# Score columns laid out by head, and batched Q/K rows in 128x32 tiles

## The chip, the cores and the metric

The kernel runs on one core of one Trainium2 chip. A core has a matrix engine (TensorE; PE in the profile, with its weight loads as PEld), three engines that work on tensors (VectorE or DVE, ScalarE or ACT, GpSimd or POOL) and a sync engine (SP) that issues most DMAs. Matmuls read SBUF and write PSUM, 128 partitions of eight banks with 512 float32 columns each; DVE and ACT bring results back to SBUF. Each engine takes its own list of instructions in order, and waits on semaphores for the others. The metric is the device time of one execution in microseconds (us).

## The reference

Two sublayers follow each other, x of shape 2048 x 512 in bfloat16. The first is attention over 64 segments of 32 rows, with a memory of 8 rows that each segment hands to the next; the second is a gated MLP that mixes rows (`_B_ref`).

```python
for s in range(n_seg):                       # 64 segments, one after the other
    xs = x[:, s * seg_len:(s + 1) * seg_len, :]
    h = concatenate([mem, xs], axis=1)       # 8 + 32 = 40 rows
    q, k, v = (einsum('btd,dhe->bhte', h, W) for W in (Wq, Wk, Wv))   # 32 heads of 128
    scores = einsum('bhqe,bhke->bhqk', q, k) * scale
    scores = where(mask, scores, -1e9)       # key < 8 or key <= query
    o = einsum('bhqk,bhke->bhqe', softmax(scores), v)
    o = einsum('bhte,hed->btd', o, Wo)
    mem = o[:, :8, :]                        # needed by the next segment
    outs.append(o[:, 8:, :])
h = x + concatenate(outs); h2 = h + _B_ref(layernorm(h), ...)
```

The memory rows make the segments sequential. All of q, k, v, the scores and the output projection of a segment's recurrent part stand on this path.

## The kernel before

Every operation is added to one list with the buffers that it reads and writes; from these the semaphore waits follow, and each engine gets its operations in the order in which they were added. So the order of the calls in the loop over segments (`for s in range(NSEG)`, L869) is the order of the work on every engine.

A segment's 40 rows are split in two groups. The first 32 (8 memory rows and the segment's first 24) are "main"; the last 8 are "extra". The extra rows do not depend on the memory, so their Q, K and V are computed in batches of 16 segments (a chunk): `qkx_mm` (L403) for Q and K, `vx_mm` (L424) for V. Chunks 0 and part of chunk 1 are done before the loop and in its first segment. The rest is spread over the loop: the list `gx` holds groups of matmuls, and each segment takes one (L942) and puts it between its V matmuls and its PV matmuls. Segments 0 to 7, 14 and 15 take a V group (L430), segments 8 to 13 and 16 to 47 a Q/K group (L411), and from segment 49 on it is a piece of the second sublayer (L725). A Q/K group has 4 heads x 4 pieces of the contraction = 16 matmuls, each with a full 128x128 weight block and 128 columns; its result is copied out by DVE (L422) after the copies of PV.

In the loop most matmuls use a quarter of the array's columns: weights of 128 rows and 32 columns, four such tiles side by side (`tile_position=(0, 32 * c)`), the four writing to the four groups of 32 partitions of one bank. The profile gives these as 128*32. PV uses the other split, 32 rows and 128 columns (32*128). The order on PE in a segment:

1. Q and K of the main rows (L481) for both halves b of the heads; ACT copies each to `Tst` (L488), and DVE transposes it to `QT` and `KT` (L494, L497).
2. `S_half(s, 0)`: for four groups of partitions c, a matmul that writes the mask (L511, identity times `mask`), then scores of main keys (L520), then scores of the extra keys (L526), all into one bank. ACT takes the exponential (L534) into `E_sb`.
3. V of half 0 (L575, 16 matmuls), then the sums of half 0 (L541 for main keys, L546 for extra keys; the matrix `ones` sums over partitions). ACT turns the sums into reciprocals by a logarithm (L553) and an exponential (L557).
4. `S_half(s, 1)`, three quarters of V of half 1 (12 matmuls of L575), the sums of half 1, the last quarter of V (4 matmuls). ACT copies V of half 1 (L582); DVE multiplies `E_sb` by the reciprocals (L561 main keys, L566 extra keys) for both halves.
5. The group from `gx`. Then PV of half 0 and half 1 (L592 main keys, L598 extra keys).
6. PV's results are copied to `cT`; the output projection follows (L625, with L676 for the extra rows of earlier segments), then the memory rows of the next segment (L649, L654).

In the score bank the 224 columns of a half lie in two blocks: columns 0 to 159 hold main keys, 40 queries for each of 4 heads; columns 160 to 223 hold extra keys. Extra keys are needed only for 16 queries of a head (the extra rows and the memory rows), 4 x 16 = 64 columns. `mask` has the same 224 columns, and the mask matmul, which opens the sum in the bank, covers them all.

## Time and profile before

| | us |
|---|---|
| median of 3 runs (lowest, highest) | 892.15 (890.42, 892.38) |
| the profiled execution | 891.1 |
| span of its instructions | 889.4 |
| PE busy | 862.0 |
| DVE busy, ACT busy, POOL busy | 487.4, 455.5, 110.7 |

The granted clock of the profiled execution is 0.994 of full speed. A row of a timeline has start, length, engine, line, operation, output and input tiles, shapes and the count of merged instructions; in brackets stands the idle time of the engine before it and what ended it ("issue" where nothing in the profile was waited for). A matmul's end is modelled, and matmuls overlap, so times between starts tell more than lengths. A row by stretches has from and to, the length, then for PE, PEld, DVE, ACT and POOL the busy time and the number of instructions, the granted clock, the share of the DMA engines and GB/s. A row on a DMA queue has the queue, its kind, packets, MB and the share of the DMA engines.

### The profile page before, as it was taken

To read this page: it belongs to the slowest core of one execution; us is meant where nothing else is said; L and a number is where in the kernel's file an instruction comes from. 1 tells how busy PE (TensorE), PEld (TensorE's weight loads), DVE (VectorE), ACT (ScalarE), POOL (GpSimd) and SP (SyncE) were. 2 spreads that over 40 slices of the span, in tenths; PEclk is the share of its full clock that TensorE was granted. 3 is DMA by queue.
4 is the path that set the end of the run, shared out by engine and by line. 5 is a ranking of instruction groups with operands and counts; after the bars stand their busy time and mean duration, and the time that the engine had idled before them with its cause. 6 is when DMAs were issued, how large, how long until landed. Compare 5 with 4: busy or idle time off the path is not lost.

```text
span 889.4 us, 46102 instructions
## 1 busy us (share of the span) xinstructions
PE 862.0 (97%) x21213; PEld 487.0 (55%) x21213; DVE 487.4 (55%) x1127; ACT 455.5 (51%) x1145; POOL 110.7 (12%) x280
## 2 busy tenths in 40 slices
PE   6889999999999999999999999999999979999997
PEld 6645555555656555656665655555555534444443
DVE  3445556565656556565656565555555546464443
ACT  2346566666665666666665666565566655400000
POOL 1420111111111111010101111111101013100000
PEclk9999999999999999999999999999999999999999
DMA  9962222222320311211212122432221296032101
GB/s 326 376 180 52 63 57 60 43 60 63 60 58 25 83 45 37 60 54 43 60 42 57 49 61 79 73 73 67 65 61 56 76 273 227 1 100 76 62 13 38
DMA packets 106312, 74.55 MB, mean 84 GB/s; under 512 B 62360, under 2 KB 91616, under 8 KB 106112
## 3 DMA queue, kind: packets, MB, share of 16 engines
q1 hardware_dynamic: 105600, 71.27, 28.8%
q8 instruction: 168, 2.75, 1.3%
q14 instruction: 32, 0.26, 0.1%
q0 software_dynamic: 192, 0.20, 0.1%
q10 hardware_dynamic: 320, 0.07, 0.0%
HBM read 41.07 MB, written 20.22 MB: 69 GB/s over the span
## 4 chain that ended last, share of the span: by engine, by line
PE 93%; DVE 2%; DMA 2%; issue 1%; POOL 1%; ACT 0%; SPq 0%; DVEq 0%
PE f_ps L481 26%; PE f_ps L625 13%; PE f_ps L575 12%; PE f_ps L1064 11%; PE f_ps L411 7%; PE f_ps L676 4%; PE f_ps L592 3%; PE f_ps L430 3%; PE f_ps L1153 3%; PE f_ps L1057 2%; PE f_ps L725 2%; PE f_ps L520 2%; PE f_ps L541 1%; PE f_ps L511 1%; DMA f_arena<-in_B_w_in_dram 1%; PE f_ps L649 1%
## 5 line engine op out<-in xcount | busy, mean ns | idle before, releaser
L481 PE MATMUL f_ps<-f_arena,f_hT 128*32 128x512 bf16 x4096 | 240.5, 380 | 1.0 <-issue 0.4
L488 ACT ACTIVATE f_Tst<-f_ps 128x512 bf16<-128x512 f32 x256 | 145.9, 596 | 78.6 <-PE f_ps L481 78.3
L481 PEld LDWEIGHTS f_ps<-f_arena,f_hT 128*32 128x32 bf16 x4096 | 93.6, 96 | 104.6 <-ACT f_hT L654 33.3
L575 PE MATMUL f_ps<-f_arena,f_hT 128*32 128x512 bf16 x2048 | 140.4, 378 | 0.0
L625 PE MATMUL f_ps<-f_arena,f_cT 128*32 128x256 bf16 x4096 | 127.4, 272 | 0.8 <-ACT f_cT L611 0.8
L625 PEld LDWEIGHTS f_ps<-f_arena,f_cT 128*32 128x32 bf16 x4096 | 99.8, 96 | 24.1 <-ACT f_cT L611 22.1
L494 DVE STREAM_TRANSPOSE f_QT<-f_Tst 128x256 uint32<-128x256 uint32 x128 | 57.0, 445 | 92.4 <-ACT f_Tst L488 92.4
L1064 PE MATMUL f_ps<-f_arena 128*128 128x512 bf16 x448 | 100.1, 379 | 0.0
L613 DVE TENSOR_SCALAR f_cT<-f_ps 128x320 bf16<-128x320 f32 x128 | 56.9, 486 | 39.7 <-PE f_ps L598 39.7
L497 DVE STREAM_TRANSPOSE f_KT<-f_Tst 128x256 uint32<-128x256 uint32 x128 | 57.0, 445 | 29.1 <-ACT f_Tst L488 26.3
L1064 PEld LDWEIGHTS f_ps<-f_arena 128*128 128x128 bf16 x448 | 43.7, 98 | 52.6
L411 PE MATMUL f_ps<-f_hTe,f_arena 128*128 128x128 bf16 x1024 | 68.2, 225 | 4.2 <-DVE f_arena L422 3.2
L411 PEld LDWEIGHTS f_ps<-f_hTe,f_arena 128*128 128x128 bf16 x1024 | 60.6, 101 | 14.1 <-issue 9.2
L504 POOL COPY f_QT<-f_arena 128x256 bf16<-128x256 bf16 x64 | 30.8, 481 | 298.7 <-PE f_ps L526 298.6
L611 ACT ACTIVATE f_cT<-f_ps 128x320 bf16<-128x320 f32 x128 | 49.0, 435 | 36.8 <-PE f_ps L598 36.8
L561 DVE SCALAR_TENSOR_TENSOR f_E_sb<-f_R_sb,f_E_sb 128x160 bf16<-128x160 f32 x128 | 41.6, 325 | 46.3 <-ACT f_R_sb L557 46.3
L642 DVE CAST f_part<-f_ps 128x256 bf16<-128x256 f32 x64 | 27.2, 424 | 67.0 <-PE f_ps L625 67.0
L553 ACT ACTIVATE f_R_sb<-f_ps 128x160 f32<-128x160 f32 x128 | 38.8, 303 | 38.1 <-PE f_ps L546 38.1
L575 PEld LDWEIGHTS f_ps<-f_arena,f_hT 128*32 128x32 bf16 x2048 | 45.1, 95 | 21.1
L654 ACT ACTIVATE f_hT<-f_ps 128x16 bf16<-128x16 f32 x126 | 23.1, 183 | 55.4 <-PE f_ps L649 55.1
L633 POOL COPY f_cTx<-f_cT 128x256 bf16<-128x256 bf16 x64 | 25.6, 401 | 195.6 <-DVE f_cT L613 195.6
L1070 DVE TENSOR_TENSOR f_arena<-f_ps,f_arena 128x512 f32<-128x512 f32 x28 | 19.3, 689 | 55.8 <-PE f_ps L1064 55.8
(106 smaller groups left out, 1160.3 us busy)
## 6 DMA issues: line engine op xcount, KB each, us to landing
wT_d<-f_wst SPq DMA_DIRECT2D x32, 256.0 KB, 2.1
f_arena<-wT_d SPq DMA_DIRECT2D x32, 256.0 KB, 5.1
f_arena<-in_A_Wq_dram SPq DMA_DIRECT2D x4, 1024.0 KB, 8.5
f_arena<-in_A_Wk_dram SPq DMA_DIRECT2D x4, 1024.0 KB, 14.1
f_arena<-in_A_Wv_dram SPq DMA_DIRECT2D x4, 1024.0 KB, 14.5
f_arena<-in_A_Wo_dram SPq DMA_DIRECT2D x4, 1024.0 KB, 13.6
f_Vx<-vext_d SPq DMA_DIRECT2D x62, 64.0 KB, 2.8
vext_d<-f_Vs SPq DMA_DIRECT2D x24, 128.0 KB, 2.0
```

What stands on the lines that cost most here:

```text
L411: pe(lambda e, h=h, dc=dc, hh=hh: e.matmul(ps[:, bank, hh * 128:(hh + 1) * 128], lhsT=ws[:, dc, h * DH:(h + 1) * DH], rhs=hTe[:, ck % 3, d ...
L481: pe(lambda e, dc=dc, c=c, rhs=rhs: e.matmul(ps[32 * c:32 * c + 32, bank, :], lhsT=hT[:, sl, dc, :], rhs=rhs, start=(dc == 0), stop=(dc == ...
L488: act(lambda e: e.activation(out=Tst[:, tb, :].rearrange("p (hp i r) -> p hp i r", i=32, r=2), in_=ps[:, bank, :].rearrange("p (hp r i) -> ...
L494: dve(lambda e: e.transpose(out=dst, in_=src), reads=[("T", tb)], writes=[("QT", b)])
L497: dve(lambda e: e.transpose(out=dst, in_=src), reads=[("T", tb)], writes=[("KT", b)])
L553: act(lambda e: e.activation(out=R_sb[:, b, :], in_=ps[:, bank, 224:384], func=ACT.Ln, scale=LNS), reads=[PB(bank)], writes=[("R", b)])
L561: dve(lambda e: e.scalar_tensor_tensor(out=E_sb[:, b, 0:160], in0=R_sb[:, b, :], scalar=RK, in1=E_sb[:, b, 0:160], op0=ALU.mult, op1=ALU.m ...
L575: pe(lambda e, dc=dc, c=c, c0=c0: e.matmul(ps[32 * c:32 * c + 32, bank, :], lhsT=hT[:, sl, dc, :], rhs=w_v[:, dc, c0:c0 + 512], start=(dc ...
L611: act(lambda e: e.activation(out=dst, in_=src, func=ACT.Copy, scale=UNSC), reads=[PB(PVB[c])], writes=[("cT", c)])
L613: dve(lambda e: e.tensor_scalar(out=dst, in0=src, scalar1=UNSC, scalar2=None, op0=ALU.mult), reads=[PB(PVB[c])], writes=[("cT", c)])
L625: pe(lambda e, h=h, g=g, i=i, b=b, c=c: e.matmul(ps[32 * g:32 * g + 32, bank, 0:d1 - d0], lhsT=cTh[:, i, 8:40], rhs=w_o[:, h, d0:d1], star ...
L1064: pe(lambda e: e.matmul(ps[:, bank, 0:TB], lhsT=z2[:, sc, fb * 128:(fb + 1) * 128], rhs=wTb[tb % 2][:, :, sc, :], start=(n == 0), stop=(n ...
```

## The change

Two things change, both in the loop over segments.

First, the score columns are laid out by head: each of the 4 heads of a half has 56 columns, 40 for main keys and behind them 16 for extra keys. The queries that see extra keys lie so that the masked columns of a head, 24 + 16, stand together: columns 16 to 55 of its 56. `mask` shrinks to 160 columns, and the mask matmul writes only these four runs of 40; the columns 0 to 15 of a head, which have no masked entry, are written first by the score matmuls. All that reads or writes scores by kind of key (L520, L526, L541, L546, L561, L566, L592, L598 of before) now does so in four runs with a step of 56 columns. The exponential still covers 224 columns.

Second, the Q/K groups in the loop use `qkx_narrow` in place of `qkx_mm`: the weight block of each matmul is split into four tiles of 32 columns, so a group has 64 matmuls of 128*32 (and 64 weight loads) in place of 16 of 128*128. The groups before the loop and in its first segment keep `qkx_mm`.

```diff
-    mask = sb("mask", [128, 224], BF)
+    mask = sb("mask", [128, 160], BF)
...
-            m1 = mask[q, 0:160].rearrange("p (g t) -> p g t", t=40)[:, :, 16:40]
+            m1 = mask[q, :].rearrange("p (g t) -> p g t", t=40)[:, :, 0:24]
...
-            m2 = mask[q, 160:224].rearrange("p (g t) -> p g t", t=16)
+            m2 = mask[q, :].rearrange("p (g t) -> p g t", t=40)[:, :, 24:40]
...
+    def qkx_narrow(ck, i, bank):
+        mi, h0 = i // 8, 4 * (i % 8)
+        ws = (w_q, w_k)[mi]
+        for hh in range(4):
+            for dc in range(DC):
+                for c in range(4):
+                    w0 = (h0 + hh) * DH + 32 * c
+                    pe(lambda e, dc=dc, hh=hh, c=c, w0=w0: e.matmul(
+                        ps[32 * c:32 * c + 32, bank, hh * 128:(hh + 1) * 128], lhsT=ws[:, dc, w0:w0 + 32], rhs=hTe[:, ck % 3, dc, :],
+                        start=(dc == 0), stop=(dc == DC - 1), tile_position=(0, 32 * c)),
+                       reads=[("hTe", ck % 3), ("W", mi, (h0 + hh) // 8)], writes=[PB(bank)])
...
-            pe(lambda e, q=q, c=c: e.matmul(ps[q, bank, 0:224], lhsT=ident[:, q], rhs=mask[:, :], start=True, stop=False,
+            pe(lambda e, q=q, c=c: e.matmul(ps[q, bank, 0:224].rearrange("p (g t) -> p g t", t=56)[:, :, 16:56], lhsT=ident[:, q],
+                                            rhs=mask[:, :].rearrange("p (g t) -> p g t", t=40), start=True, stop=False,
...
-                    ps[32 * c:32 * c + 32, bank, g * 40:(g + 1) * 40], lhsT=KT[:, b, hp, :, r], rhs=QT[:, b, hp, :, r],
+                    ps[32 * c:32 * c + 32, bank, g * 56:g * 56 + 40], lhsT=KT[:, b, hp, :, r], rhs=QT[:, b, hp, :, r],
...
-                ps[32 * c:32 * c + 32, bank, 160:224], lhsT=QTx[buf][:, 1, j, h0:h0 + 4, :].rearrange("p h k -> p (h k)"),
+                ps[32 * c:32 * c + 32, bank, 0:224].rearrange("p (g t) -> p g t", t=56)[:, :, 40:56], lhsT=QTx[buf][:, 1, j, h0:h0 + 4, :].rearrange("p h k -> p (h k)"),
...
+    def E_main(b, q=slice(0, 128)):
+        return E_sb[q, b, :].rearrange("p (g t) -> p g t", t=56)[:, :, 0:40]
+
+    def E_ext(b, q=slice(0, 128)):
+        return E_sb[q, b, :].rearrange("p (g t) -> p g t", t=56)[:, :, 40:56]
...
-            qkx_mm(ck, i, XB)
+            qkx_narrow(ck, i, XB)
```

In the sums, the normalisations and PV, `E_sb[:, b, 0:160]` becomes `E_main(b)`, and `E_sb[:, b, 160:224]` becomes `E_ext(b)`.

More of the change, by code (lines that the diff above doesn't have):

```diff
@@ L540, in sm_sums @@
             q = slice(32 * c, 32 * c + 32)
-            pe(lambda e, q=q, c=c: e.matmul(ps[q, bank, 224:384], lhsT=ones[:, q], rhs=E_sb[:, b, 0:160], start=True, stop=False,
+            pe(lambda e, q=q, c=c: e.matmul(ps[q, bank, 224:384].rearrange("p (g q) -> p g q", q=40), lhsT=ones[:, q], rhs=E_main(b),
+                                            start=True, stop=False,
                                             skip_group_check=True, tile_position=(0, 32 * c)),
@@ L546, in sm_sums @@
             pe(lambda e, q=q, c=c: e.matmul(ps[q, bank, 224:384].rearrange("p (g q) -> p g q", q=40)[:, :, 0:16], lhsT=ones[:, q],
-                                            rhs=E_sb[:, b, 160:224].rearrange("p (g q) -> p g q", q=16), start=False, stop=True,
+                                            rhs=E_ext(b), start=False, stop=True,
                                             skip_group_check=True, tile_position=(0, 32 * c)),
@@ L560, in sm_norm @@
     def sm_norm(b):
-        dve(lambda e: e.scalar_tensor_tensor(out=E_sb[:, b, 0:160], in0=R_sb[:, b, :], scalar=RK, in1=E_sb[:, b, 0:160],
+        dve(lambda e: e.scalar_tensor_tensor(out=E_main(b), in0=R_sb[:, b, :].rearrange("p (g q) -> p g q", q=40), scalar=RK, in1=E_main(b),
                                              op0=ALU.mult, op1=ALU.mult),
             reads=[("R", b), ("E", b)], writes=[("E", b)])
-        ev = E_sb[:, b, 160:224].rearrange("p (g q) -> p g q", q=16)
+        ev = E_ext(b)
         rv = R_sb[:, b, :].rearrange("p (g q) -> p g q", q=40)[:, :, 0:16]
@@ L592, in PV_half @@
                 pe(lambda e, q=q, c=c, g=g, c0=c0: e.matmul(
-                    ps[:, PVB[c], c0:c0 + 40], lhsT=V_sb[q, b, g * 128:(g + 1) * 128], rhs=E_sb[q, b, g * 40:(g + 1) * 40],
+                    ps[:, PVB[c], c0:c0 + 40], lhsT=V_sb[q, b, g * 128:(g + 1) * 128], rhs=E_sb[q, b, g * 56:g * 56 + 40],
                     start=(g == 0), stop=False, skip_group_check=True, tile_position=(32 * c, 0)),
@@ L599, in PV_half @@
                 ps[:, PVB[c], 160 * b:160 * b + 160].rearrange("p (g q) -> p g q", q=40)[:, :, 0:16], lhsT=Vx[q, xb, b, :],
-                rhs=E_sb[q, b, 160:224].rearrange("p (g q) -> p g q", q=16),
+                rhs=E_ext(b, q),
                 start=False, stop=True, skip_group_check=True, tile_position=(32 * c, 0)),
```

## The prediction

> **What bounds the kernel now.** I read the page first (busy times, queues, costliest groups), then the timeline of single iterations of the segment loop, then counts of PE's instructions by stretch beside the DMA queue of kind "instruction". The page:

> ```profile
> span 889.4 us, 46102 instructions
> PE 862.0 (97%) x21213; PEld 487.0 (55%) x21213; DVE 487.4 (55%) x1127; ACT 455.5 (51%) x1145; POOL 110.7 (12%) x280
> L411 PE MATMUL f_ps<-f_hTe,f_arena 128*128 128x128 bf16 x1024 | 68.2, 225 | 4.2 <-DVE f_arena L422 3.2 <-ACT f_V_sb L582 1.0
> ```

> PE is busy for 97% of the span, so cheaper matmuls look like time. But a matmul row lasts some 200 ns beyond its issue, and a wait shorter than that leaves no idle time. Starts have to be read instead. One iteration (segment 37) from the mask to PV, columns start, length, engine, line:

> ```profile
> 511.55 0.27 PE L511 MATMUL f_ps<-f_mask,f_ident 128*32 128x224 bf16 x4
> 511.64 0.27 PE L520 MATMUL f_ps<-f_QT,f_KT 128*32 128x40 bf16 x16
> 511.75 0.20 PE L526 MATMUL f_ps<-f_QT,f_arena 128*32 128x64 bf16 x4
> 511.77 0.60 ACT L488 ACTIVATE f_Tst<-f_ps 128x512 bf16<-128x512 f32 x1 [0.27 <-PE f_ps L481]
> 511.77 1.03 PE L575 MATMUL f_ps<-f_arena,f_hT 128*32 128x512 bf16 x16
> ...
> 512.26 0.35 ACT L534 ACTIVATE f_E_sb<-f_ps 128x224 bf16<-128x224 f32 x1
> 512.40 0.45 DVE L497 STREAM_TRANSPOSE f_KT<-f_Tst 128x256 uint32<-128x256 uint32 x1 [0.42 <-ACT f_Tst L488]
> ...
> 512.67 0.25 PE L541 MATMUL f_ps<-f_E_sb,f_ones 128*32 128x160 bf16 x4
> ...
> 512.75 0.20 PE L546 MATMUL f_ps<-f_E_sb,f_ones 128*32 128x64 bf16 x4
> ...
> 512.78 0.27 PE L511 MATMUL f_ps<-f_mask,f_ident 128*32 128x224 bf16 x4
> ...
> 512.90 0.28 PE L520 MATMUL f_ps<-f_QT,f_KT 128*32 128x40 bf16 x16
> ...
> 513.05 0.82 PE L575 MATMUL f_ps<-f_arena,f_hT 128*32 128x512 bf16 x12
> ...
> 513.70 0.25 PE L541 MATMUL f_ps<-f_E_sb,f_ones 128*32 128x160 bf16 x4
> ...
> 513.81 0.39 PE L575 MATMUL f_ps<-f_arena,f_hT 128*32 128x512 bf16 x4
> ...
> 514.13 1.07 PE L411 MATMUL f_ps<-f_hTe,f_arena 128*128 128x128 bf16 x16
> ...
> 514.62 0.58 ACT L582 ACTIVATE f_V_sb<-f_ps 128x512 bf16<-128x512 f32 x1
> ...
> 514.99 0.22 DVE L566 SCALAR_TENSOR_TENSOR f_E_sb<-f_R_sb,f_E_sb 128x64 bf16<-128x64 f32 x1
> 515.13 0.27 PE L592 MATMUL f_ps<-f_E_sb,f_V_sb 32*128 32x40 bf16 x16
> ...
> 515.38 0.28 PE L592 MATMUL f_ps<-f_E_sb,f_V_sb 32*128 32x40 bf16 x16
> ```

> Three starts hang on other engines. The first sums (L541, 512.67) come 0.06 after the exponential ends (512.26 + 0.35), which itself follows ACT's copy L488, not the scores. The second scores (L520, 512.90) come 0.05 after the transpose of K ends (512.40 + 0.45). The second PV (515.38) needs L582 (ends 515.20) and L566 (ends 515.21). So this stretch is a chain through ACT and DVE with PE laid tightly around it.

> **The mask matmul, 224 to 160 columns, 128 groups of four.** Four of 224 take 0.09 (511.55 to 511.64), four of 160 take 0.08 (L541 to L546, 512.67 to 512.75); by the columns it would be 0.09 x 160/224 = 0.065. Saved: 0.01 to 0.025 a group, 1.3 to 3.2 us in all, if it reached the end. It doesn't. In the first half the sixteen V matmuls behind it take 0.90 (511.77 to 512.67), where twelve take 0.65 (513.05 to 513.70), so sixteen need 0.87: PE already waits 0.03 for the exponential. In the second half the mask takes 0.12 until L520 starts, instead of 0.09: PE already waits 0.03 for K's transpose. Both savings lengthen these waits. I take 0; if the covers were gone, -1.3 to -3.2.

> Score and extra columns in runs of 40 and 16 instead of contiguous blocks: L546 already writes four runs of 16 and takes 0.03 (512.75 to 512.78) as L526 does with a contiguous block (511.75 to 511.77). L566 already reads R in runs; it takes 0.22 for 64 columns. I take 0 for PE, ACT (same 224 columns) and DVE. At worst the two normalisations on the chain lose 0.02 each, 64 x 0.04 = 2.6 us; at best nothing. The smaller memsets and selects on POOL lie in the start-up, beside PE work.
> [...]

> **The batched rows, 16 matmuls 128x128 to 64 of 128x32, in 38 iterations** (segments 8 to 13 and 16 to 47; 26 groups of the start keep the old form). Now 0.32 passes between the last V matmuls and L411 (513.81 to 514.13) and 1.00 in L411. An iteration with L430 in that place, 128x32 like its neighbours, and a row of just the new shape:

> ```profile
> 107.17 0.25 PE L541 MATMUL f_ps<-f_E_sb,f_ones 128*32 128x160 bf16 x4
> ...
> 107.28 0.39 PE L575 MATMUL f_ps<-f_arena,f_hT 128*32 128x512 bf16 x4
> 107.49 1.04 PE L430 MATMUL f_ps<-f_arena,f_hTe 128*32 128x512 bf16 x16
> ...
> 108.81 0.28 PE L592 MATMUL f_ps<-f_E_sb,f_V_sb 32*128 32x40 bf16 x16
> ```

> ```profile
> 414.08 0.40 PE L376 MATMUL f_ps<-f_ident,f_xn 128*32 128x128 bf16 x16
> 414.32 0.61 PE L481 MATMUL f_ps<-f_arena,f_hT 128*32 128x512 bf16 x8
> ```

> Without the change of array form V's last four take 0.21 (107.28 to 107.49): 0.11 saved. Sixteen of the new shape take 0.24, so 64 take at most 0.96, against 1.00. Starts do not limit them: sixteen L520 start within 0.11 (511.64 to 511.75), 7 ns each. PE would reach the first PV 0.11 to 0.15 earlier, 38 x that = 4.2 to 5.7 us. But the second PV starts 1.64 after the sums in the L430 iteration (107.17 to 108.81) and 1.68 in segment 37 (513.70 to 515.38): 1.64 is the chain. What is late next is L582/L566, and only 0.04 is left: 38 x 0.04 = **-1.5 us**.
> [...]

> **What the change adds: 96 instructions on PE's queue in each of the 38 iterations** (48 matmuls, 48 weight loads). PE's instructions arrive by DMA:

> ```profile
> q8 instruction: 77, 1.26, 1.6%
> 233.00:554.00 321.00, 320.85 (x9716) 193.72 (x9710) 190.75 (x464) 198.24 (x519) 38.57 (x92) 1.00 0.20 52
> 164.26 0.29 PE L376 MATMUL f_ps<-f_ident,f_xn 128*32 128x128 bf16 x6 [0.60 <-issue]
> 206.37 0.24 PE L376 MATMUL f_ps<-f_ident,f_xn 128*32 128x128 bf16 x4 [0.49 <-issue]
> 0.00:161.66 161.66, 147.75 (x3968) 93.38 (x3972) 82.20 (x191) 82.58 (x203) 29.74 (x90) 0.99 0.52 158
> 0.00:163.46 163.46, 149.55 (x4042) 95.02 (x4042) 83.07 (x192) 83.17 (x205) 30.14 (x91) 0.99 0.51 156
> 0.00:205.67 205.67, 191.16 (x5316) 119.80 (x5316) 107.78 (x252) 109.41 (x273) 35.25 (x103) 0.99 0.44 132
> 0.00:501.10 501.10, 485.93 (x14212) 297.10 (x14216) 282.10 (x675) 291.83 (x749) 70.86 (x187) 1.00 0.31 86
> 0.00:503.40 503.40, 488.23 (x14304) 298.30 (x14308) 283.68 (x678) 293.48 (x754) 71.34 (x188) 1.00 0.31 86
> 0.00:505.36 505.36, 490.19 (x14368) 299.88 (x14372) 284.60 (x682) 294.70 (x758) 71.34 (x188) 1.00 0.31 86
> 0.00:511.50 511.50, 496.33 (x14524) 303.36 (x14528) 288.87 (x691) 298.36 (x766) 72.53 (x191) 1.00 0.30 85
> 561.41 0.40 PE L481 MATMUL f_ps<-f_arena,f_hT 128*32 128x512 bf16 x4 [0.24 <-issue]
> ```

> In 321 us, 77 packets came for 19,426 counted instructions: 252 each, 256 with the stand-alone waits that these columns leave out. PE twice sat idle in the middle of L376 with nothing to wait for ("issue"). Before the two stalls stand 8084 and 10,632 instructions: 2548 apart, ten packets. So these are late packets. The packet of the first was recorded at 161.66, with 144 instructions left before it (7940 to 8084), and PE went on at 164.26: 2.60 us. The packet of the second was recorded at 203.74, 2.63 before PE went on; that of a later one (561.41) at 558.50, 2.91 before. Counted on by 256 from these borders, the packets of the 321 us start with 211 instructions left on average. These must last as long as a packet needs.

> Differences of the count in segment 36: from the mask (501.10) to the last V matmuls (503.40) 184 instructions in 2.30 us, 80 per us; to PV's end (505.36) 128 in 1.96, 65 per us; to the next mask 312 in 6.14, 51 per us. The densest 211 are the 184 and 27 beside them: 2.30 + 27/65 = 2.7 us, just enough, hence few stalls. With 96 more and 0.04 less, the middle stretch has 224 in 1.92, 117 per us, and 211 of these last 1.80.

> An iteration of some 720 instructions is no multiple of 256, so a border passes through all places. Take 2.7 us for a packet. For a border p instructions into the middle stretch the 211 before it last p/117 + (211-p)/80: 2.53 at p = 27 (0.17 short), 1.80 at 211 (0.90 short), and so to 224. Behind it each instruction adds 1/51 - 1/117 = 0.011, so the shortage is gone after 81. Area: 184 x (0.17 + 0.90)/2 + 13 x 0.90 + 81 x 0.90/2 = 146; over 256: 0.57 us an iteration, 38 x 0.57 = **+22 us**. In the same way 2.6 us give 0.47 (+18) and 2.9 us give 0.82 (+31). If PE's queue asks for packets earlier when they run out faster, it falls towards 0; a gain is excluded, since more instructions never need fewer packets. I take 2.7, because the changed iterations lie between the stalls of 2.6 and that of 2.9. Nothing hides such a stall: from PV to the next mask PE leads.

> **Sum.** Profiled execution 891.1 (span 889.4, 1.7 around it): 0 - 1.5 + 22 = 911.6. The median of the runs, 892.15, lies 1.05 above: 913.

> **Rivals.**
> - *Packets keep up.* The queue asks earlier, and only the cover shrinks: 892.15 - 1.5 = 890.6, no change that can be measured. For it: just a few stalls now, with an average of 4.2 us between packets (321/77). Against it: those stalls. It decides if 211 instructions in 1.80 us bring no "issue" rows.
> - *Faster.* The second PV's chain gives way, because the shorter mask lets the second exponential and all behind it start earlier. All savings count: -3.2 - 4.9 = 884. It decides if L582 and L566 end 0.1 earlier against L541. Against it: K's transpose ends at 512.85 whatever the mask does.

> **Chances.** Late packets 0.80, packets keep up 0.13, faster 0.07. About 0.2% (1.8 us) is what a measurement tells from no change. Faster 0.09, same 0.11, slower 0.80 (of "packets keep up" 0.02 lie beyond the bound and count as faster). Predicted 913. The likeliest case alone has 900 to 925 (892 and 8 to 33: below, half of the 18 less the 1.5; above, 31 and the 2.6 of the normalisations). With "packets keep up" the range is 890 to 925.

> **What the profile after would show.** Right: idle times ended by "issue", of 0.3 to 0.9 us, in the new group, in PV or soon behind it, in about half of the 38 iterations; the instruction queue's packets up by 38 x 96/256 = 14; the changed iterations, 10.40 now from 501.10 to 511.50, near 10.9 on average; segments 0 to 7 and 48 to 63 unchanged; L541 still 0.06 after the exponential. Wrong: if the changed iterations last 10.36, packets keep up; below 10.28, the chain reading fails; if the second L520 starts earlier against the end of K's transpose, so does the zero for the mask.

## The result and the profile after

The changed kernel takes 931.06 us (median of 6 runs, 926.02 to 933.09); the kernel before, run beside it, takes 891.61 us (6 runs, 889.84 to 892.38). The ratio is 1.043, with a 95% interval of 1.041 to 1.045. The kernel became slower, as forecast, but by 39 us where 21 were predicted; 931 lies above the range. The profiled execution after took 933.1 us, at a granted clock of 0.992. The lines have moved by 12 to 20: L481 is now L493, L520 is L533, L541 is L560, L575 is L595, L592 is L612, L625 is L645; the new group is L422 and its copy by DVE L434.

Rows of the page after (span, PE's busy time, the instruction queue, the chain of waits, two groups of instructions):

```profile
span 931.4 us, 49743 instructions
PE 871.2 (94%) x23030; PEld 490.3 (53%) x23037; DVE 487.2 (52%) x1127; ACT 455.7 (49%) x1145; POOL 110.6 (12%) x280
q8 instruction: 183, 3.00, 1.4%
PE 89%; issue 4%; DMA 2%; DVE 2%; SPq 1%; POOL 1%; ACT 0%; DVEq 0%
L645 PE MATMUL f_ps<-f_arena,f_cT 128*32 128x256 bf16 x4096 | 133.9, 274 | 13.8 <-issue 12.2
L612 PE MATMUL f_ps<-f_E_sb,f_V_sb 32*128 32x40 bf16 x2048 | 37.8, 178 | 12.8 <-issue 11.2
```

and the rows of before that answer to three of them:

```profile
q8 instruction: 168, 2.75, 1.3%
PE 93%; DVE 2%; DMA 2%; issue 1%; POOL 1%; ACT 0%; SPq 0%; DVEq 0%
L625 PE MATMUL f_ps<-f_arena,f_cT 128*32 128x256 bf16 x4096 | 127.4, 272 | 0.8 <-ACT f_cT L611 0.8
```

DVE, ACT and POOL do the same work. PE's span grew by 42 us and its busy time by 9; most of the rest is idle time ended by "issue" (4% of the chain), and it stands where the code was not touched: in the output projection (L645) and PV (L612), both behind the new group. The two stretches of changed iterations (segments 8 to 13 and 16 to 47, from mask to mask), as the sums of a view by stretches, first before, then after:

```profile
sum 395.54, PE 394.79 PEld 238.14 DVE 235.35 ACT 244.62 POOL 48.42; mean PE 197.40 PEld 119.07 DVE 117.68 ACT 122.31 POOL 24.21
```

```profile
sum 438.23, PE 404.90 PEld 242.46 DVE 235.21 ACT 244.88 POOL 48.48; mean PE 202.45 PEld 121.23 DVE 117.61 ACT 122.44 POOL 24.24
```

They account for 42.7 us, 1.12 for each of the 38 iterations. The iterations without the change hold their time: segments 1 to 7, 14 and 15 together 93.0 (93.7 before), segments 48 to 62 154.8 (155.4 before), the start and the end within 1 us.

PE's instructions come in packets of 16 KB, one DMA each (the queue above: 183 packets, 3.00 MB). The place in PE's list where a new packet begins is called its border here. How a late packet looks in the timeline after (segment 20; new group, PV, then Q and K of the next segment):

```profile
275.78 0.25 PE L560 MATMUL f_ps<-f_E_sb,f_ones 128*32 128x160 bf16 x4
...
275.88 0.39 PE L595 MATMUL f_ps<-f_arena,f_hT 128*32 128x512 bf16 x4
...
276.10 1.07 PE L422 MATMUL f_ps<-f_hTe,f_arena 128*32 128x128 bf16 x64
...
277.10 0.22 PE L612 MATMUL f_ps<-f_E_sb,f_V_sb 32*128 32x40 bf16 x8
...
278.06 0.22 PE L612 MATMUL f_ps<-f_E_sb,f_V_sb 32*128 32x40 bf16 x8 [0.74 <-issue]
...
281.28 0.61 PE L493 MATMUL f_ps<-f_arena,f_hT 128*32 128x512 bf16 x7
...
282.53 0.39 PE L493 MATMUL f_ps<-f_arena,f_hT 128*32 128x512 bf16 x1 [0.64 <-issue]
```

PE stops after eight of sixteen PV matmuls, and again after seven of eight Q matmuls, for about 1 us each, with nothing to wait for. The new group itself runs without a stop here. Now counts of instructions from the start of the span (a view by stretches of after; add the counts of PE and PEld), to the start of an instruction packet's DMA and to the stall that this packet ends, for three packets:

```profile
0.00:255.41 255.41, 234.24 (x6948) 144.04 (x6952) 132.01 (x312) 134.67 (x338) 39.98 (x115) 0.99 0.41 118
0.00:257.00 257.00, 235.25 (x6974) 144.76 (x6974) 132.45 (x312) 135.06 (x339) 40.28 (x115) 0.99 0.41 117
0.00:275.72 275.72, 252.30 (x7528) 154.41 (x7528) 142.11 (x334) 146.09 (x368) 42.28 (x120) 0.99 0.39 112
0.00:277.90 277.90, 253.91 (x7612) 155.64 (x7612) 143.04 (x338) 147.44 (x371) 42.44 (x120) 0.99 0.39 112
0.00:279.41 279.41, 255.26 (x7664) 156.57 (x7668) 143.70 (x340) 148.18 (x373) 42.44 (x120) 0.99 0.39 112
0.00:282.30 282.30, 257.74 (x7739) 158.16 (x7739) 145.55 (x343) 148.78 (x375) 42.84 (x121) 0.99 0.39 112
```

Before the stalls stand 13,948, 15,224 and 15,478 instructions: 1276 apart (five packets, at 255 to the packet) and 254 apart (one). When the DMA of the packet began, only 48, 168 and 146 instructions were left to run. In segments 8 to 47 there are 58 places ("stalls") where PE starts nothing for more than 0.3 us. 50 of them lie at the same place of a packet, at its border: counted with PE's stand-alone semaphore instructions, which the trace has and the columns above leave out, all 50 come 193 to 195 instructions behind a multiple of 256. So a packet holds 256, about one of them such a wait (114 in the 107 packets from the first of the 50 to the last). The other eight last 0.31 to 0.40. Of the 50, 5 lie in the new group, 14 in L612, 19 in L645 and the rest elsewhere. They last 0.31 to 1.67 and add up to 44.8 us, counted from start to start, so that the ordinary spacing is in it. Before there were two at borders, 1.5 us.

One part of the 42.7 us is not itself waiting. Right behind the stall of 1.67 in segment 13 the granted clock was 0.50 for 3.4 us (199.3 to 202.7), and this iteration lasts 13.66. With the narrow group alone (below) the same segment lasts 11.72 at a clock of 1.00. That the stall set off the lower clock is not shown.

### The profile page after: what moved, and what is told of

Read it like the earlier page. It is cut to its first block, busy times and chain, and to the rows that moved or that the text cites. A ratio compares the mean times of both kernels' runs of the same rounds, so it can differ in the third digit from the quotient of the medians.

```text
span 931.4 us, 49743 instructions
## 1 busy us (share of the span) xinstructions
PE 871.2 (94%) x23030; PEld 490.3 (53%) x23037; DVE 487.2 (52%) x1127; ACT 455.7 (49%) x1145; POOL 110.6 (12%) x280
## 4 chain that ended last, share of the span: by engine, by line
PE 89%; issue 4%; DMA 2%; DVE 2%; SPq 1%; POOL 1%; ACT 0%; DVEq 0%
PE f_ps L493 24%; PE f_ps L645 13%; PE f_ps L595 12%; PE f_ps L1084 10%; PE f_ps L422 4%; PE f_ps L696 3%; PE f_ps L612 3%; PE f_ps L442 3%; PE f_ps L1173 3%; PE f_ps L1077 2%; PE f_ps L745 2%; PE f_ps L411 2%; PE f_ps L533 2%; PE f_ps L560 2%; PE f_ps L523 1%
## 5 line engine op out<-in xcount | busy, mean ns | idle before, releaser
L493 PE MATMUL f_ps<-f_arena,f_hT 128*32 128x512 bf16 x4096 | 241.4, 380 | 2.4 <-issue 1.8
L493 PEld LDWEIGHTS f_ps<-f_arena,f_hT 128*32 128x32 bf16 x4096 | 94.1, 96 | 106.0 <-ACT f_hT L674 33.2
L645 PE MATMUL f_ps<-f_arena,f_cT 128*32 128x256 bf16 x4096 | 133.9, 274 | 13.8 <-issue 12.2
L595 PE MATMUL f_ps<-f_arena,f_hT 128*32 128x512 bf16 x2048 | 140.3, 378 | 0.0
L645 PEld LDWEIGHTS f_ps<-f_arena,f_cT 128*32 128x32 bf16 x4096 | 102.0, 97 | 41.0 <-ACT f_cT L631 22.5
L595 PEld LDWEIGHTS f_ps<-f_arena,f_hT 128*32 128x32 bf16 x2048 | 44.9, 95 | 21.3
L660 ACT ACTIVATE f_part<-f_ps 128x256 bf16<-128x256 f32 x64 | 24.5, 383 | 55.2 <-PE f_ps L645 55.2
L612 PE MATMUL f_ps<-f_E_sb,f_V_sb 32*128 32x40 bf16 x2048 | 37.8, 178 | 12.8 <-issue 11.2
```

Source lines behind the costliest of these rows:

```text
L493: pe(lambda e, dc=dc, c=c, rhs=rhs: e.matmul(ps[32 * c:32 * c + 32, bank, :], lhsT=hT[:, sl, dc, :], rhs=rhs, start=(dc == 0), stop=(dc == ...
L595: pe(lambda e, dc=dc, c=c, c0=c0: e.matmul(ps[32 * c:32 * c + 32, bank, :], lhsT=hT[:, sl, dc, :], rhs=w_v[:, dc, c0:c0 + 512], start=(dc ...
L612: pe(lambda e, q=q, c=c, g=g, c0=c0: e.matmul(ps[:, PVB[c], c0:c0 + 40], lhsT=V_sb[q, b, g * 128:(g + 1) * 128], rhs=E_sb[q, b, g * 56:g * ...
L645: pe(lambda e, h=h, g=g, i=i, b=b, c=c: e.matmul(ps[32 * g:32 * g + 32, bank, 0:d1 - d0], lhsT=cTh[:, i, 8:40], rhs=w_o[:, h, d0:d1], star ...
```

## The experiments

The theory at this point: the time goes into instruction packets that come too late, and what counts is how many PE instructions the loop has. Rivals: the layout in runs costs time; the 128x32 form of the group costs time in itself (its own length, or what it does to its neighbours); the chain behind PV.

**Layout and mask alone.** The changed kernel, with the groups in the loop as before:

```diff
-            qkx_narrow(ck, i, XB)
+            qkx_mm(ck, i, XB)
```

> The new score layout and the mask of 160 columns, with the batched Q/K rows in the loop as before (16 matmuls of 128x128). Theory 'late instruction packets': the whole loss comes from the 96 added instructions of a Q/K group, so this is the kernel before within 1.5 us, 890 to 893, and the second L520 still starts 0.05 after K's transpose. Rival 'layout': runs of 40 and 16 columns slow the matmuls or the normalisations on the chain; then 895 to 931, with every iteration of the loop longer by up to 0.6 us. Rival 'mask saves': 3 us faster, 888.

Measured: 891.30 us against 891.50, ratio 0.9997 (0.9985 to 1.001). The changed iterations' sum, and an iteration without a stall (segment 36):

```profile
sum 394.94, PE 394.94 PEld 236.63 DVE 234.99 ACT 244.84 POOL 48.68; mean PE 197.47 PEld 118.31 DVE 117.49 ACT 122.42 POOL 24.34
```

```profile
427.97 0.24 PE L523 MATMUL f_ps<-f_mask,f_ident 128*32 128x160 bf16 x4
428.04 0.27 PE L533 MATMUL f_ps<-f_QT,f_KT 128*32 128x40 bf16 x16
...
428.69 0.35 ACT L553 ACTIVATE f_E_sb<-f_ps 128x224 bf16<-128x224 f32 x1
428.82 0.45 DVE L509 STREAM_TRANSPOSE f_KT<-f_Tst 128x256 uint32<-128x256 uint32 x1 [0.42 <-ACT f_Tst L500]
429.09 0.25 PE L560 MATMUL f_ps<-f_E_sb,f_ones 128*32 128x160 bf16 x4
...
429.20 0.24 PE L523 MATMUL f_ps<-f_mask,f_ident 128*32 128x160 bf16 x4
...
429.33 0.28 PE L533 MATMUL f_ps<-f_QT,f_KT 128*32 128x40 bf16 x16
...
430.12 0.25 PE L560 MATMUL f_ps<-f_E_sb,f_ones 128*32 128x160 bf16 x4
...
430.23 0.39 PE L595 MATMUL f_ps<-f_arena,f_hT 128*32 128x512 bf16 x4
...
430.56 1.07 PE L411 MATMUL f_ps<-f_hTe,f_arena 128*128 128x128 bf16 x16
...
431.56 0.27 PE L612 MATMUL f_ps<-f_E_sb,f_V_sb 32*128 32x40 bf16 x16
...
431.81 0.28 PE L612 MATMUL f_ps<-f_E_sb,f_V_sb 32*128 32x40 bf16 x16
```

The mask now passes in 0.07 (427.97 to 428.04) instead of 0.09. The first sums still come 0.05 after the exponential (428.69 + 0.35), 1.12 after the mask, as before (511.55 to 512.67). The second scores start 0.06 after K's transpose (428.82 + 0.45), and the second mask takes 0.13 until then, where it took 0.12. From the first mask to the second sums 2.15 pass, as before. So the saving turns into waiting, and the runs cost nothing: with runs of 16 and 40 columns throughout, no slowing of the matmuls is seen (the sixteen scores have a row of 0.27, as before; the changed iterations add up to 394.94 against 395.54).

**The narrow group alone.** Before's layout, with `qkx_narrow` in the loop:

```diff
-            qkx_mm(ck, i, XB)
+            qkx_narrow(ck, i, XB)
```

> The old layout and mask, with 64 matmuls of 128x32 in the loop's Q/K groups. 'Late packets': 926 to 933 like the changed kernel, with idle PE only at places a multiple of 256 instructions apart. 'Layout': near 892.

Measured: 927.13 us against 891.50, ratio 1.040 (1.037 to 1.043). The sum of the changed iterations, and the instruction queue of its page:

```profile
sum 432.61, PE 403.38 PEld 242.49 DVE 235.34 ACT 244.89 POOL 48.48; mean PE 201.69 PEld 121.24 DVE 117.67 ACT 122.44 POOL 24.24
```

```profile
q8 instruction: 183, 3.00, 1.4%
```

The loss is that of the narrow group: 47 stalls at packet borders, 40.0 us in all. The 4 us between this kernel and the full change are not explained by the layout, which costs nothing alone. In the changed iterations of the two profiled executions they are 5.6 us (438.23 against 432.61). Some 1.9 of these lie in segment 13 with its stretch at half the clock (13.66 against 11.72). For the rest, borders fall on other instructions in the two kernels, so other packets are late; that this makes up the rest is argued, not shown.

**The old form in more instructions.** Two experiments keep the weight block of 128x128 and cut the moving 128 columns, into two halves (32 matmuls, 32 more PE instructions an iteration) and into four quarters (64 matmuls, 96 more, as many as in the change):

```diff
+                for c in range(2):      # second kernel: range(4), 32 columns
-                   ps[:, bank, hh * 128:(hh + 1) * 128] ... rhs=hTe[:, ck % 3, dc, :]
+                   ps[:, bank, hh * 128 + 64 * c:hh * 128 + 64 * (c + 1)] ... rhs=hTe[:, ck % 3, dc, 64 * c:64 * (c + 1)]
```

> The kernel before, each matmul of the loop's Q/K groups cut into two with 64 columns of the moving operand: 32 of 128x128 with the same weights loaded twice, same array form as before, 32 instructions more an iteration, about the same PE time. 'Late packets', with the rule read from the changed kernel's trace that 256 instructions must last 3.6 us: 4 to 19 us more, near 10, so 902. Rival 'tiles' (128x32 tiles, or the passage from them to PV's 32x128, are slow by themselves): the form is as before, so 892.

> As the cut into two, but four matmuls of 32 columns: 64 of 128x128, the same 96 added instructions as in the changed kernel without its tiles. 'Late packets': at least 30 us more than before, 922 to 945, with idle PE a multiple of 256 instructions apart; a little more if the short matmuls take longer than 0.89 together. 'Tiles': 892 plus only what the short matmuls take by themselves, and no idle PE.

Measured: halves 898.39 us against 891.50, ratio 1.008 (1.006 to 1.010); quarters 929.34 us, ratio 1.043 (1.040 to 1.045). The sums of the two, and the group of quarters in the timeline:

```profile
sum 399.21, PE 397.93 PEld 241.24 DVE 235.46 ACT 244.94 POOL 48.64; mean PE 198.96 PEld 120.62 DVE 117.73 ACT 122.47 POOL 24.32
```

```profile
sum 435.20, PE 426.31 PEld 269.10 DVE 235.35 ACT 244.81 POOL 48.51; mean PE 213.15 PEld 134.55 DVE 117.68 ACT 122.41 POOL 24.26
...
331.85 1.77 PE L422 MATMUL f_ps<-f_hTe,f_arena 128*128 128x32 bf16 x64
333.55 0.27 PE L605 MATMUL f_ps<-f_E_sb,f_V_sb 32*128 32x40 bf16 x16
```

The halves lose 3.7 us in the changed iterations, with 5 stalls of 3.0 us, and one more of 1.1 us in segment 48, behind them, which lasts 12.94 (10.71 before); right behind that stall the granted clock was 0.51 for 3.4 us (562.5 to 565.9). The quarters lose as much as the change, but for another reason, and the test is not the clean one that was meant: their group takes 1.70 (331.85 to 333.55), not 1.00, and pushes PV back by 0.7 in every iteration, 27 us in 38. Only 20 stalls of 13.3 us come on top. That they are fewer fits the longer group, which spreads the same number of instructions over more time. So equal totals prove nothing about the cause here; the stalls had to be counted.

**The narrow group in every second iteration.** Before's layout, with 19 narrow groups and 19 wide ones:

```diff
-            qkx_mm(ck, i, XB)
+            (qkx_narrow if i % 2 else qkx_mm)(ck, i, XB)
```

> The kernel before, with 64 matmuls of 128x32 in every second Q/K group of the loop (19 of 38). 'Late packets': 907 to 920; the loss is uneven, iterations with a split group from 10.33 us (where no packet's border falls badly) to 12, and some with an unsplit group are longer too, as their packet is asked for late. 'Tiles': 19 x 1.1 = 21 us as well, 913, but every split iteration near 11.4 and every unsplit one at 10.37. From the split iterations without idle PE the trace tells what the form alone is worth: 10.33 if the chain behind the second PV sets the end (0.04 less than before), 10.25 if not.

Measured: 909.17 us against 892.40, ratio 1.019 (1.016 to 1.021). The sum of the changed iterations, and a narrow one (segment 19) that no packet delays ahead of PV:

```profile
sum 413.75, PE 399.13 PEld 240.06 DVE 235.53 ACT 245.11 POOL 48.71; mean PE 199.56 PEld 120.03 DVE 117.76 ACT 122.56 POOL 24.36
```

```profile
257.07 0.25 PE L553 MATMUL f_ps<-f_E_sb,f_ones 128*32 128x160 bf16 x4
...
257.17 0.39 PE L587 MATMUL f_ps<-f_arena,f_hT 128*32 128x512 bf16 x4
...
257.39 1.07 PE L422 MATMUL f_ps<-f_hTe,f_arena 128*32 128x128 bf16 x64
...
258.39 0.27 PE L604 MATMUL f_ps<-f_E_sb,f_V_sb 32*128 32x40 bf16 x16
...
258.71 0.28 PE L604 MATMUL f_ps<-f_E_sb,f_V_sb 32*128 32x40 bf16 x16
```

Half the groups cost 18.2 us, in 26 stalls of 21.1 us. That is about half of the 37.1 that all 38 cost in this layout (432.61 less 395.54), so the total doesn't tell the rivals apart; the single iterations do. Some narrow iterations last 10.36 (segment 19) and 10.64 (31), others 11.95 (17); some wide ones are longer too (46: 11.37). That a border in one iteration makes the next packet late in another would explain these; it is not shown. A form that is slow in itself would cost the same each time. The pair also shows what the form saves without late packets: from the second sums to the first PV 1.32 here (257.07 to 258.39) against 1.44 with the wide group (430.12 to 431.56, shown above); to the second PV 1.64 against 1.69. Medians over the iterations of this one run: 1.32 and 1.43, 1.64 and 1.68.

**Tiles of 64 columns.** Before, with 32 matmuls in 128x64 tiles, side by side in pairs; 32 more instructions, as with the halves, but in the column tiles' form:

```diff
-            qkx_mm(ck, i, XB)
+            qkx_64(ck, i, XB)      # as qkx_narrow, c in range(2), 64 columns, tile_position=(0, 64 * c)
```

> The kernel before, with the loop's Q/K groups in 32 matmuls of 128x64 tiles, two side by side: 32 instructions more an iteration. 'Late packets': like the cut into two of 64 columns, 896 to 902. 'Tiles': half the way of the changed kernel or more, 910 to 931.

Measured: 899.66 us against 892.40, ratio 1.007 (1.005 to 1.009):

```profile
sum 405.12, PE 399.08 PEld 240.24 DVE 235.62 ACT 244.75 POOL 48.52; mean PE 199.54 PEld 120.12 DVE 117.81 ACT 122.38 POOL 24.26
```

14 stalls, 9.9 us; iterations without one last 10.38. The whole run stands as far from before as with the halves, the changed iterations not quite (9.6 us here, 3.7 there, with one more stall behind them in segment 48). So tiles of 64 columns stay far below the 910 that was put down for a cost of the column form. But 14 stalls here and 5 there, for the same number of added instructions, mean that the number alone doesn't set the size. Where the borders fall is the likely reason; a small share of the form is not excluded.

**More instructions somewhere else.** Nothing of the change at all: before, with the 64 matmuls of 256 columns of the output projection cut into 128 of 128 columns in segments 16 to 47, 128 more PE instructions in each of 32 iterations.

```diff
-        Wo((0, 2, 1, 3), OB, 0, OC)
+        wp = 2 if 16 <= s < 48 else 1
+        Wo((0, 2, 1, 3), OB, 0, OC, wp)      # wp matmuls of 256 / wp columns, same weights
```

> The kernel before with nothing changed in masks, scores or Q/K groups; in segments 16 to 47 each matmul of the output projection (64 a segment, 128x32 tiles, 256 columns) is cut into two of 128 columns: 128 instructions more in each of 32 iterations, PE time about the same (0.04 us more an iteration by the start spacing). 'Late packets', 256 instructions must last 3.6 us: 930 to 945, with idle PE a multiple of 256 instructions apart, mostly in or behind the projection. 'Tiles' or 'layout': 892 to 894.

Measured: 938.17 us against 892.40, ratio 1.051 (1.048 to 1.054). The stretches of segments 8 to 13 (not cut) and 16 to 47 (cut), and the projection's group:

```profile
136.99:199.19 62.20, 62.20 (x1900) 37.38 (x1896) 37.69 (x93) 39.00 (x102) 7.72 (x18) 1.00 0.22 54
219.84:594.65 374.81, 342.64 (x12120) 211.27 (x12116) 197.85 (x481) 206.18 (x538) 40.93 (x96) 1.00 0.20 47
```

```profile
L627 PE MATMUL f_ps<-f_arena,f_cT 128*32 128x128 bf16 (+1 forms) x6144 | 134.0, 238 | 15.8 <-issue 14.8
```

The uncut segments take 10.37 each; the cut ones 11.71 on average (374.81 / 32), 42.3 us in all above before's 332.5. PE's busy time in them grows from 332.35 to 342.64 only; 35 stalls at packet borders hold 41.1 us. This shows the cause: with layout, mask and Q/K groups as before, instructions added in another place cost the same kind of time.

No kernel among these beats the one before. Not tried: what sets the time that a packet takes (other traffic on the DMA engines, where the instructions lie in memory).

## Why the prediction was right, and why its size was wrong

*The mask: 0. Right.* The experiment with layout and mask alone shows both waits in place and longer, and no change of the time.

*The layout in runs: 0. Right*, by the same run; neither the 2.6 us at worst for the normalisations nor anything for PE appeared.

*The form of the group: 0.11 to 0.15 earlier at the first PV, 0.04 kept. Right up to the second PV.* Measured 0.11 and 0.04 in the run with every second group. The new group is not shorter from its first start to PV (276.10 to 277.10, 1.00, as L411's 430.56 to 431.56); what is saved is the change of array form ahead of it (0.22 from the last V matmuls, 0.33 with L411). The 1.5 us themselves can't be read off, since the shortest narrow iteration, 10.36 long against 10.37 with the wide group, still has a pause of 0.13 at a border in the projection.

*96 more instructions: late packets, +22 us. Right in kind, mis-sized.* This is the step that failed: the loop lost 42.7 us, 1.12 an iteration, where 0.57 was worked out. The mechanism showed all the signs that were named (idle ended by "issue" in PV and behind it, 15 more packets for the 14 forecast, the unchanged segments unchanged, L560 still behind the exponential), but not in half of the iterations and not within 0.9 us: a late packet fell into 37 of the 38, with stalls of up to 1.67; the one iteration without, segment 8, lasts 10.51. The sum held the packet's start fixed at "211 instructions left on average", a number of the kernel before, and asked how long these 211 would last. They were not 211. In segments 8 to 47 the changed kernel had 170 left on average when a packet's DMA began, 143 at the late ones, and as few as 48. The other factor held: from the start of a late packet's DMA to PE going on 2.2 to 3.1 us passed, 2.46 in the median, near the 2.7 taken. Of this the DMA itself took 1.1 in the median, and PE went on 1.4 after its end; what fills the 1.4 is not shown.

Why fewer were left can be read from the starts. In the changed kernel a packet's DMA begins a median of 1.1 us (0.1 to 2.2) after PE passed the border one packet earlier, and in all 50 late cases both borders fall into one iteration. In 17 of them the first lies in the new group; in 33 the second, some 3 us later and too late, lies in PV or the projection. So the fetch seems to be set off by a border and not by a count of instructions that are left; in a dense burst PE has run more of its 256 by then. This reading rests on the starts alone, no run tested it by itself, and the starts fit it only roughly: in the kernel before, 4 of 99 DMAs began up to 0.5 us ahead of that border. The right question was how long 256 instructions last from border to border, not how long 211 last to the border. For late packets it was 3.7 us in the median (2.8 to 4.5), about the 1.1 and the 2.5 together. As a check, the starts of before, with L411's 16 pairs replaced by 64 in 0.89 us and with no two borders allowed closer than 3.6 us, give 39 us more than before's own starts under the same rule; 19 with half the groups, 44 with the projection cut. Measured over the 38 iterations: 42.7 (37.1 in before's layout), 18.2, 41.5. With 32 pairs the rule gives 8, and the runs gave 3.7 and 9.6. The 3.6 was chosen to fit before and after, so the agreement of these two is no evidence; that of the others is, some. With 3.5 or 3.7 the 39 becomes about 35 or 44.

In the terms of the prediction: it expected 39% of the packets of an iteration to be late (278 places of 720), by 0.53 on average; 46% were late (50 of 108), by 0.9. The upper end of its range, 31 us from a packet of 2.9, varied the factor that held and left out the one that didn't. The rival that the queue asks earlier when instructions run out faster, with the chance of 0.13, fell: in segments 8 to 47 of the changed kernel no packet's DMA began ahead of the border before it, and the median start lay 1.1 us behind that border against 0.8 in the kernel before: later, not earlier. The rival that the second PV's chain gives way fell with the 1.64 that stayed. One reading was loose without harm to the sum: stand-alone waits make up only about one of the four instructions by which 252 a packet falls short of 256. Five packets hold 1276 counted ones, 255 each; the rest is where the ends of the 321 us cut the packets.

## What to carry to other kernels

In this loop the count of PE instructions was a cost of its own: in the four kernels with the most late packets, 256 instructions took 3.6 to 3.8 us in the median where a packet was late, about 70 in a microsecond. The loop before used 629 in 10.39 us (segments 16 to 47), 61 in a microsecond, a mean below that with bursts above it. With 96 more in the same time the mean itself would be 70, so nothing was left to make up for the bursts. Before a matmul is cut into more and smaller ones, look at the instruction queue in the profile, count the instructions from border to border in the densest stretch, and look for idle times ended by "issue" that lie a multiple of one packet apart; here 45 of the 50 lay outside the new group. A number that belongs to the old rhythm, such as the instructions left when a packet starts, must be worked out anew for the new one.
